# Attention's turns as pairs of 64 rows, the tail's second half an iteration later, ranks moved to other iterations

## The chip, the cores and the metric

The kernel runs on one core of a Trainium2 chip. The metric is the device time of one execution in microseconds (us). Five engines work side by side, each through its own queue in order: TensorE (PE, with its weight loads shown as PEld), VectorE (DVE), ScalarE (ACT), GpSimd (POOL) and SyncE (SP), which issues most DMAs. Matmuls write PSUM, and VectorE and ScalarE read it.

## The reference

Attention with a threshold under the row's maximum, then a gated mixture of experts (two of eight), then a dense layer of 2048 hidden units.

```python
scores = scale * np.matmul(q, k.transpose(0, 1, 3, 2))          # 4 batches, 8 heads, 576 x 576
thresh = np.max(scores, axis=-1, keepdims=True) - tau
scores = np.where(scores >= thresh, scores, -1000000000.0)
attn = np.exp(scores - np.max(scores, axis=-1, keepdims=True))
attn = attn / (np.sum(attn, axis=-1, keepdims=True) + 1e-09)
x = np.matmul(attn, v)                                          # 2304 tokens x 512
...
noisy_logits = x @ w_gate + np.log1p(np.exp(x @ w_noise)) * noise
out[mask] += top2_w * (np.maximum(x[mask] @ w1[e], 0.0) @ w2[e])  # both chosen experts e
...
g = np.maximum(h, 0.0) + alpha * np.minimum(h, 0.0)             # h = x @ w_in
return g @ w_out
```

## The kernel before, in words

The order of all instructions is written by hand: Python loops emit them, and each engine works through its own in that order.

Attention goes through 80 units (`units`). A unit is one pair of heads (`hp`) and one chunk of 128 queries of one batch, both heads of it, or a "t" unit: the 64 queries that are left over, with the two heads stacked on the 128 partitions (`nh(i)` is 2 or 1). The first 16 units are batch 0's chunks with the pair of heads as the outer loop (`SOLO`); from there on four units in a row, one for each pair, make up one tile of 128 tokens.

The main loop runs over iterations `i` and overlaps units: in iteration `i` the scores of unit `i+1` are multiplied (`s_mm`, two heads side by side in two halves of 64 rows of the array), the minimum of the negated scores of unit `i` is taken on VectorE (`d1`, `L358`), ScalarE takes the exponential (`a1`, `L369`) and the threshold (`thresh`), VectorE masks unit `i-1` (`d2`, `L382`), the masked exponentials of unit `i-2` (`it`) are turned on TensorE (`t_mm`: nine 128x128 transposes in a full unit, five in a "t" unit) and copied from PSUM by ScalarE (`a2`), and the outputs of unit `i-3` (`iv`) are multiplied (`pv`). The ninth turn is the "tail": the last 64 keys of both heads.

PSUM tiles of the tag "t" (`psum_t`) come from three buffers, which the turns, the turned rows of a finished token tile, its logits, their flip and the ranks share. A buffer is taken when its last reader is done.

Around a finished token tile the list `x_stages` places four steps in later iterations: `rows` (four turns, multiplied by 1/sum on VectorE, `L477`, and stored), `logits` (four small matmuls), `flip` (one turn) and `sum_`. The list `gating` does the same for groups of two or three tiles: noise, top two, `rank` (five matmuls of ones and a triangle), `place`, and the sends (`send`, indirect DMAs). An entry `(d, p, f)` means: `d` iterations later, at place `p`, where 0 is ahead of the outputs and 1 behind them.

ScalarE also rounds the next q and k (`split_hi`, `L289` and `L291`) and, from iteration 66 on, expert weights (`w_hi`, `L170`). Behind attention the experts and the dense layer follow, with TensorE working without pause.

Of the kernel before, what the change touches and what calls it, by code (L numbers as in the profile page):

```python
# [10 lines left out]
OP = mybir.AluOpType  # L11
# [22 lines left out]
def emit(tc, qt, kt, v, tau, wg, wn, noise, w1, w2, w_in, w_out, alpha, out):  # L34
# [8 lines left out]
    with (  # L43
# [192 lines left out]
        wcat, noise_t = cr([HP, 32]), cr([NT, E])  # L236
        lt_ring = Ring([cr([128]) for _ in range(3)])
# [10 lines left out]
        def load_consts():  # L248
            for h in range(2):
                for k, w in enumerate((wg, wn)):  # L250
                    sp.dma_start(wcat[h * 64:h * 64 + 64, :, h * 16 + k * 8:h * 16 + k * 8 + 8],
                                 w.rearrange("(c h p) e -> h p c e", h=2, p=64)[h])
            sp.dma_start(noise_t, noise)
            sp.dma_start(alpha_t, alpha)
# [134 lines left out]

        def t_mm(i, part):  # L390
            u = st[i]
            em = u["em"]
            emf = em.rearrange("p h s -> p (h s)")
            ps = psum_t()
            u["pt", part] = ps
            if part < 2:
                o = part * 640
                for j in range(4):
                    pe.transpose(ps[:, j * 128:j * 128 + 128], emf[:, o + j * 128:o + j * 128 + 128], ident)
            elif nh(i) == 2:  # L400
                pe.transpose(ps[:, :128], emf[:, 512:640], ident)
            else:
                pe.transpose(ps[:64, :128], emf[:, 512:576], ident)

        def a2(i, part):
            u = st[i]
            if part == 0:
                u["P"] = pt_ring()
            ps = u.pop(("pt", part))
            if part < 2:  # L410
                act.copy(u["P"][:, 4 * part:4 * part + 4].rearrange("p a b -> p (a b)"), ps)
            elif nh(i) == 2:
                act.copy(u["P"][:, 8], ps[:, :128])
            else:
                act.copy(u["P"][:64, 8], ps[:64, :128])
# [49 lines left out]
        def x_stages(T):  # L465
            g = {}

            def rows():
                x = xts[T]
                e = esum[T]  # L470
                dve.tensor_scalar(e, e, 1e-9, None, op0=OP.add)
                dve.reciprocal(e, e)
                ps = psum_t()
                for c in range(HP):
                    pe.transpose(ps[:, c * 128:c * 128 + 128], x[:, c], ident)
                xtok[T] = xtok_ring()
                dve.tensor_tensor(xtok[T].rearrange("p (h d) -> p h d", h=H), ps.rearrange("p (h d) -> p h d", h=H),  # L477
                                  e[:, :, None].to_broadcast([128, H, D]), op=OP.mult)
                sp.dma_start(xd[T * 128:T * 128 + 128], xtok[T])

            def logits():
                x = xts[T]
                ps = psum_t()
                for c in range(HP):
                    pe.matmul(ps[c * 32:c * 32 + 32, :128], wcat[:, c], x[:, c], start=True, stop=True,
                              skip_group_check=True)
                g["lt"] = lt_ring()
                act.copy(g["lt"], ps[:, :128])

            def flip():  # L490
                g["ps"] = psum_t()
                pe.transpose(g["ps"][:, :128], g["lt"], ident)

            def sum_():
                t = lt_ring()
                dve.tensor_tensor(t.rearrange("p (h j) -> p h j", h=H),
                                  g["ps"][:, :128].rearrange("p (h j) -> p h j", h=H),
                                  esum[T][:, :, None].to_broadcast([128, H, 16]), op=OP.mult)
# [10 lines left out]
        def gating(t0, t1):  # L509
# [90 lines left out]
            if 3 < t1 <= 12:  # L600
                plan = [(d, 1, f) for d, f in enumerate(first)] + [(5, 1, rank), (6, 0, place)]
                if t1 == FIRST:
                    plan.append((9, 0, close))
                return plan + [(6 + q, 1, lambda a=a: send(*a)) for q, a in enumerate(sends)]
            if t1 <= 15:
                plan = [(d // 2, 1, f) for d, f in enumerate(first)] + [(4, 1, rank), (5, 0, place)]
                return plan + [(5 + q // 2, 1, lambda a=a: send(*a)) for q, a in enumerate(sends)]
# [103 lines left out]
        for i in range(END):  # L711
            it, iv = i - DT, i - DT - 1
            tiles, outs = 0 <= it < NU, 0 <= iv < NU
            if tiles:
                t_mm(it, 0)
                a2(it, 0)
            if i < NU:
# [17 lines left out]
            if i + 1 < NU:  # L735
                s_mm(i + 1)
# [392 lines left out]
```

## Time and profile before

| | |
|---|---|
| timed runs | 1195.02, 1197.77 and 1198.08 us, median 1197.77 |
| the profiled execution's own time | 1204.04 us, of which its span (first to last instruction) is 1202.3 us |
| TensorE, matmuls | 1163.5 us busy, 97% of the span |
| VectorE, ScalarE, GpSimd | 588.4, 528.8 and 509.8 us busy |
| mean granted TensorE clock | 0.995 |

A busy time counts each moment in which at least one instruction of the engine ran. Matmuls overlap, and their ends are modelled, so a busy TensorE is not one at its peak. Line numbers such as L399 are those of the kernel before.

### The profile page before, as it was taken

Reading aid. Unit: us, or ns where it says so; the run is one execution under the profiler, and the core shown is the slowest. Engines: PE = TensorE matmul, PEld = TensorE weight load, DVE = VectorE, ACT = ScalarE, POOL = GpSimd, SP = SyncE. Lnnn points to the kernel's source line nnn. Section 1 sums busy time; section 2 is a strip of 40 time slices with the busy share of each in tenths; the row PEclk is TensorE's granted clock in tenths of the full one; section 3 lists DMA queues with packets and bytes.
Section 4 is the critical chain, followed back from the end, with each engine's and each line's share of the span. In section 5 each row is a group of like instructions: output and inputs, shape, how many; then the busy total and the mean of one; then the engine's idle time right before and its main releaser. Section 6 shows DMA issues by size and latency. Waiting matters only on the chain. (4 is left out here: it accounts for less than half of the span.)

```text
span 1202.3 us, 20313 instructions
## 1 busy us (share of the span) xinstructions
PE 1163.5 (97%) x7942; PEld 999.8 (83%) x7942; DVE 588.4 (49%) x1287; ACT 528.8 (44%) x1039; POOL 509.8 (42%) x553
## 2 busy tenths in 40 slices
PE   7998989999889999999999999999999999999997
PEld 6887777877778989888989898989888888888886
DVE  7978878799533433432534342345333333333222
ACT  7977868787524444444444354433111211211111
POOL 6736435643224544444444445546323332332221
PEclk9999999999999999999999999999999999999999
DMA  7323222142235555455555545542110100200001
GB/s 216 130 84 130 78 92 62 72 148 80 108 131 185 184 190 196 166 166 176 201 189 188 187 164 180 192 153 72 37 34 18 62 26 18 71 19 18 35 1 37
DMA packets 60597, 135.19 MB, mean 112 GB/s; under 512 B 9680, under 2 KB 10320, under 8 KB 60496
## 3 DMA queue, kind: packets, MB, share of 16 engines
q1 hardware_dynamic: 54448, 114.61, 28.1%
q0 software_dynamic: 5760, 18.88, 4.6%
q8 instruction: 64, 1.05, 0.3%
q14 instruction: 37, 0.30, 0.1%
q10 hardware_dynamic: 288, 0.34, 0.1%
HBM read 93.96 MB, written 39.85 MB: 111 GB/s over the span
## 5 line engine op out<-in xcount | busy, mean ns | idle before, releaser
L197 PE MATMUL ps_t<-m_v,m_pair 128*128 128x384 f32 (+2 forms) x1216 | 220.8, 318 | 1.2 <-DVE m_gate L208 1.2
L197 PEld LDWEIGHTS ps_t<-m_v,m_pair 128*128 128x128 f32 x1216 | 187.0, 190 | 9.8 <-DVE m_gate L208 1.8
L173 POOL TENSOR_TENSOR m_pair<-m_v,m_pair 128x1024 fp32r<-128x1024 f32 x55 | 134.8, 2452 | 137.8 <-ACT m_pair L170 137.5
L215 PE MATMUL ps_s<-m_pair,m_hh 128*128 128x512 f32 x528 | 175.6, 396 | 0.0
L954 DVE TENSOR_SCALAR m_tmp<-ps_t,alpha_t 128x512 f32<-128x512 f32 (+1 forms) x80 | 55.7, 696 | 216.9 <-PE ps_t L197 216.9
L208 DVE SCALAR_TENSOR_TENSOR m_gate<-ps_t,m_hh 128x384 fp32r<-128x384 f32 (+1 forms) x120 | 58.3, 493 | 153.8 <-ACT m_hh L207 153.7
L197 PE MATMUL ps_t<-m_v,m_early 128*128 128x256 f32 (+2 forms) x672 | 127.5, 321 | 1.3 <-ACT m_v L189 0.8
L382 DVE SCALAR_TENSOR_TENSOR m_hh<-m_tmp,sm,m_hh 128x576 f32<-128x576 f32 x144 | 127.2, 915 | 2.4 <-ACT sm L363 2.0
L215 PEld LDWEIGHTS ps_s<-m_pair,m_hh 128*128 128x128 f32 x528 | 99.2, 188 | 20.3
L959 POOL TENSOR_TENSOR m_v<-m_tmp,m_v 128x512 fp32r<-128x512 f32 x39 | 50.3, 1290 | 149.1 <-ACT m_v L958 149.1
L358 DVE TENSOR_SCALAR_CACHE_REDUCE m_tmp<-ps_s 128x576 f32<-128x576 f32 x144 | 103.6, 752 | 18.5 <-PE ps_s L347 15.8
L197 PEld LDWEIGHTS ps_t<-m_v,m_early 128*128 128x128 f32 x672 | 105.8, 189 | 6.6 <-ACT m_v L189 1.1
L369 ACT ACTIVATE m_hh<-m_tmp,sm 128x576 f32<-128x576 f32 x144 | 105.7, 783 | 10.9 <-DVE m_tmp L358 10.8
L347 PE MATMUL ps_s<-m_pair 64*128 64x288 f32 (+1 forms) x864 | 96.1, 321 | 12.9 <-DVE m_tmp L358 8.2
L215 PE MATMUL ps_s<-m_pair,m_gate 128*128 128x512 f32 x264 | 103.2, 391 | 0.0
L958 ACT CAST m_v<-m_tmp 128x512 fp32r<-128x512 f32 x39 | 24.2, 621 | 177.1 <-DVE m_tmp L955 177.1
L347 PEld LDWEIGHTS ps_s<-m_pair 64*128 64x128 f32 (+1 forms) x864 | 73.2, 194 | 27.9 <-DVE m_tmp L358 13.7
L978 PE MATMUL ps_s<-m_pair,m_v 128*128 128x512 f32 x396 | 95.9, 391 | 0.0
L207 ACT ACTIVATE m_hh<-ps_t 128x384 fp32r<-128x384 f32 (+1 forms) x120 | 51.9, 439 | 93.5 <-PE ps_t L197 92.2
L959 POOL TENSOR_TENSOR m_gate<-m_tmp,m_gate 128x512 fp32r<-128x512 f32 (+1 forms) x41 | 44.1, 1077 | 114.5 <-ACT m_gate L958 110.3
L978 PE MATMUL ps_s<-m_pair,m_gate 128*128 128x512 f32 x360 | 89.2, 393 | 0.0
L978 PEld LDWEIGHTS ps_s<-m_pair,m_v 128*128 128x128 f32 x396 | 73.9, 188 | 15.3
(226 smaller groups left out, 1994.2 us busy)
## 6 DMA issues: line engine op xcount, KB each, us to landing
m_v<-in_w_dram SPq DMA_DIRECT2D x64, 512.0 KB, 4.0
yg<-m_tmp SPq DMA_DIRECT2D x40, 256.0 KB, 3.6
m_tmp<-in_w_in_dram SPq DMA_DIRECT2D x16, 512.0 KB, 5.2
m_tmp<-in_w_out_dram SPq DMA_DIRECT2D x16, 512.0 KB, 5.7
m_v<-xg SPq DMA_DIRECT2D x20, 256.0 KB, 6.2
m_rows<-xg SPq DMA_DIRECT2D x20, 256.0 KB, 4.1
m_early<-in_kt_dram SPq DMA_DIRECT2D x15, 320.0 KB, 3.1
yg<-m_gate SPq DMA_DIRECT2D x18, 256.0 KB, 2.0
```

Of the source, the lines that this page charges most:

```text
L173: eng.tensor_tensor(WL[n], wraw.pop(n), f32(WH[n]), op=OP.subtract)
L197: pe.matmul(ps[:, :n], w[wc[d]][:, col:col + 128], x[xx][:, d, :n], start=(k == 0), stop=(k == 11))
L207: act.activation(h, ps, AF.Relu)
L208: dve.scalar_tensor_tensor(hs[1][:, f * n:f * n + n], ps, 0.0, f32(h), op0=OP.max, op1=OP.subtract)
L215: pe.matmul(ps, a[:, o:o + 128], ww[w][:, c:c + 512], start=(f == 0 and k == 0), stop=(f == nf - 1 and k == 2))
L347: pe.matmul(u["ps", h][:, x, :288], lhs, kk[r, o:o + 288], start=(k == 0), stop=(k == 2))
L358: dve.tensor_scalar(u["sp"][:, h].rearrange("p (a b) -> p a b", a=2), ps[:, :, :288], -0.125, None, op0=OP.mult, op1=OP.min, accum_out=u[" ...
L369: act.activation(u["em"][:, h], u["sp"][:, h], AF.Exp, bias=u["sm"][:, h:h + 1], scale=-1.0)
L382: dve.scalar_tensor_tensor(u["em"][:, h], u["sp"][:, h], sm[:, 2 + h:3 + h], u["em"][:, h], op0=OP.is_le, op1=OP.mult, accum_out=acc)
L954: dve.tensor_scalar(g, ps, 0.0, alpha_t[:, f:f + 1], op0=OP.min, op1=OP.mult)
L959: pool.tensor_tensor(h[:, n:2 * n], g, f32(h[:, :n]), op=OP.subtract)
L978: pe.matmul(ps, h[x][:, t * 128:t * 128 + 128], ww[w][:, c:c + 512], start=(f == 0 and k == 0), stop=(f == 15 and k == 2))
```

## The change

Every turn in attention is done as two turns of 64 rows each, side by side in the two row halves of the array, the way the scores are: `lo` gets queries 0 to 63, `hi` queries 64 to 127, in two PSUM tiles. All of a unit's turns are emitted at the start of the iteration and the scores right behind them. The tail's first half (`tail`) is turned there too, the second half, in the same PSUM tile, one iteration later (`t_mm(iv, 1)`), and copied then (`a2(iv, 2)`). The token tile's rows and the flip are turned in the same way and move ahead of the outputs. The logits take two steps of 64 columns in place of four of 32. Ranks come four iterations after their gating starts, with `place`.

```diff
+        def turn2(lo, hi, src):
+            r0, r1 = slice(0, 64), slice(64, 128)
+            pe.transpose(lo, src[r0], ident[r0, r0])
+            pe.transpose(hi, src[r1], ident[r1, r1])
...
         def t_mm(i, part):
...
-                for j in range(4):
-                    pe.transpose(ps[:, j * 128:j * 128 + 128], emf[:, o + j * 128:o + j * 128 + 128], ident)
...
+            if part == 0:
+                lo, hi, tail = [psum_t() for _ in range(3)]
+                u["pt"] = [lo, hi, tail]
+                for j in range(4 * nh(i)):
+                    if j == 4 * nh(i) - 1:
+                        pe.transpose(tail[:k, r0], emf[r0, 512:512 + k], ident[r0, r0])
+                    o = j * 128 + (128 if j > 3 else 0)
+                    c = slice(j * 64, j * 64 + 64)
+                    turn2(lo[:, c], hi[:, c], emf[:, o:o + 128])
             else:
+                two = pe.transpose(u["pt"][2][:k, r1], emf[r1, 512:512 + k], ident[r1, r1])
+                tc.add_manual_dep(two.ins, u["copied"].ins.name, ...)
...
         def a2(i, part):
...
             if part < 2:
-                act.copy(u["P"][:, 4 * part:4 * part + 4].rearrange("p a b -> p (a b)"), ps)
+                done = act.copy(P[:, :n, part * 64:part * 64 + 64],
+                                       ps[:, :n * 64].rearrange("p (a b) -> p a b", b=64))
+                u.setdefault("copied", done)
...
-            return [(0, 1, rows), (1, 1, logits), (2, 1, flip), (3, 0, sum_)]
+            return [(0, 0, rows), (1, 1, logits), (2, 0, flip), (2, 0, sum_)]
...
-                plan = [(d, 1, f) for d, f in enumerate(first)] + [(5, 1, rank), (6, 0, place)]
+                plan = [(d // 2, 1, f) for d, f in enumerate(first)] + [(4, 0, rank), (4, 0, place)]
...
+            if outs:
+                t_mm(iv, 1)
+                a2(iv, 2)
             if tiles:
                 t_mm(it, 0)
                 a2(it, 0)
+                a2(it, 1)
...
-            if tiles and nh(it) == 2:
-                t_mm(it, 1)
-                a2(it, 1)
-            if tiles:
-                t_mm(it, 2)
-                a2(it, 2)
+            if i + 1 < NU:
+                s_mm(i + 1)
```

The first place is TensorE's queue in an iteration of the first 16 units. Before, the turns (`L399`, the tail `L401`) stand ahead of the scores (`L347`) and the outputs (`L435`):

```order
L399 MATMUL ps_t<-ident,m_hh 128x128 [waits DVE_49,Activation_49]
L399 MATMUL ps_t<-ident,m_hh 128x128 x3
L401 MATMUL ps_t<-ident,m_hh 128x128 [waits Activation_49]
L347 MATMUL ps_s<-m_pair 128x288 [waits DVE_49] x2
L347 MATMUL ps_s<-m_pair 128x288 x10
```

And with the change, from the tail's first half (`L409`) on, with the last pair of turns (`L395`, `L396`), the scores (`L349`), the outputs (`L448`, `L450`) and the next iteration's first instruction, the tail's second half (`L414`):

```order
L409 MATMUL ps_t<-ident,m_hh 128x64 [waits Activation_49]
L395 MATMUL ps_t<-ident,m_hh 128x64
L396 MATMUL ps_t<-ident,m_hh 128x64
L349 MATMUL ps_s<-m_pair 128x288 [waits DVE_49] x2
L349 MATMUL ps_s<-m_pair 128x288 x10
L448 MATMUL ps_v<-m_last,m_v_72 64x128 x8
L450 MATMUL ps_v<-m_last,m_v_72 64x128 x2
L414 MATMUL ps_t<-ident,m_hh 128x64 [waits Activation_49]
```

The last pair of turns now stands behind an instruction that waits for ScalarE: the wait of `L409` is for the copy of the tail before it (`L428` below), since the two have one PSUM buffer.

The second place is ScalarE's queue in the same iterations. Before, a half's copy (`L411`), the two exponentials (`L369`), the other copies (`L411`, `L413`), the threshold (`L363`), the outputs' copy (`L453`):

```order
L411 COPY m_last<-ps_t 128x512 [waits PE_49,Activation_49]
L369 ACTIVATE m_hh<-m_tmp,sm_154 128x576 [waits DVE_49] x2
L411 COPY m_last<-ps_t 128x512 [waits PE_49,Activation_49]
L413 COPY m_last<-ps_t 128x128 [waits PE_49]
L363 ACTIVATE sm_154<-sm_154,taut 128x2
L453 COPY m_last<-ps_v 128x128 [waits PE_49]
```

And with the change, a rounding of k (`L293`) ahead of it:

```order
L293 CAST m_pair<-m_early 128x640 [waits DMAHW6_49]
L428 COPY m_last<-ps_t 128x128 [waits PE_49]
L424 COPY m_tmp<-ps_t 128x8x64 [waits PE_49,Activation_49] x2
L371 ACTIVATE m_hh<-m_tmp,sm_147 128x576 [waits DVE_49] x2
L365 ACTIVATE sm_147<-sm_147,taut 128x2
L466 COPY m_hh<-ps_v 128x128 [waits PE_49]
```

The tail's copy (`L428`, of the unit before) now comes first, and both halves' copies (`L424`) stand between it and the exponentials.

The third place is TensorE's queue in an iteration with a token tile's turned rows. Before, the rows (`L475`) come behind the outputs:

```order
L347 MATMUL ps_s<-m_pair 128x288 x10
L435 MATMUL ps_v<-m_last,m_v_73 64x128 x8
L437 MATMUL ps_v<-m_last,m_v_73 64x128 x2
L475 MATMUL ps_t<-ident,m_last 128x128 [waits DVE_49]
L475 MATMUL ps_t<-ident,m_last 128x128 x3
```

And with the change (the rows are turned by `L395` and `L396` too, from `m_last` here; three more pairs follow, then the outputs):

```order
L349 MATMUL ps_s<-m_pair 128x288 [waits DVE_49] x2
L349 MATMUL ps_s<-m_pair 128x288 x10
L395 MATMUL ps_t<-ident,m_last 128x64 [waits Activation_49]
L396 MATMUL ps_t<-ident,m_last 128x64 [waits Activation_49]
```

The rows now stand between the scores and the outputs, and wait for ScalarE's copies of the low and the high half, whose PSUM buffers they take.

## Rows read from the trace of the kernel before

**Rows 1.** The page's first part: busy us, share of the span, instructions.
```profile
PE 1163.5 (97%) x7942; PEld 999.8 (83%) x7942; DVE 588.4 (49%) x1287; ACT 528.8 (44%) x1039; POOL 509.8 (42%) x553
```

**Rows 2.** Windows, five stretches: busy PE, PEld, DVE, ACT, POOL (instructions), clock, DMA.
```profile
17.91:58.53 40.62, 40.55 (x494) 34.48 (x493) 37.75 (x99) 39.62 (x94) 25.55 (x39) 1.00 0.48 156
58.53:93.11 34.58, 33.53 (x417) 28.13 (x416) 26.92 (x73) 26.50 (x66) 14.72 (x36) 1.00 0.22 73
93.11:217.26 124.15, 114.09 (x1305) 92.22 (x1305) 103.81 (x311) 94.36 (x209) 63.47 (x110) 0.99 0.27 92
217.26:240.84 23.58, 23.47 (x285) 20.11 (x284) 17.79 (x58) 18.24 (x46) 14.21 (x32) 1.00 0.18 68
240.84:301.54 60.70, 56.38 (x654) 45.45 (x653) 56.37 (x146) 48.51 (x103) 24.24 (x32) 0.97 0.33 118
```

**Rows 3.** Timeline of PE, one iteration: start, length, instruction, count [idle before].
```profile
38.54 1.05 PE L347 MATMUL ps_s<-m_pair 64*128 64x288 f32 x12
39.52 1.09 PE L435 MATMUL ps_v<-m_tmp,m_v 128*64 128x128 f32 x16
...
40.77 1.09 PE L399 MATMUL ps_t<-ident,m_hh 128*128 128x128 f32 x8
...
41.90 0.40 PE L347 MATMUL ps_s<-m_pair 64*128 64x288 f32 x2
```

**Rows 4.** Timeline of ACT, parts of two iterations of that stretch.
```profile
35.43 1.48 ACT L369 ACTIVATE m_hh<-m_tmp,sm 128x576 f32<-128x576 f32 x2
36.78 0.61 ACT L411 COPY m_tmp<-ps_t 128x512 f32<-128x512 f32 x1
37.24 0.31 ACT L413 COPY m_tmp<-ps_t 128x128 f32<-128x128 f32 x1
37.40 0.35 ACT L363 ACTIVATE sm<-sm,taut 128x2 f32<-128x2 f32 x1
37.60 0.30 ACT L453 COPY m_hh<-ps_v 128x128 f32<-128x128 f32 x1
...
41.05 0.68 ACT L289 CAST m_pair<-m_early 128x576 fp32r<-128x576 f32 x1
41.62 0.59 ACT L411 COPY m_tmp<-ps_t 128x512 f32<-128x512 f32 x1
```

**Rows 5.** Windows, a group of four units with one token tile (units 36 to 39).
```profile
131.86:147.88 16.02, 15.15 (x179) 12.37 (x178) 13.77 (x47) 13.51 (x31) 8.16 (x15) 1.00 0.17 57
```

**Rows 6.** Groups by line, 0 to 420 us: count, busy, mean ns, idle before, releasers.
```profile
L170 ACT CAST m_pair<-m_v 128x1024 fp32r<-128x1024 f32 x12 | 12.5, 1045 | 0.0
L477 DVE TENSOR_TENSOR m_gate<-ps_t,es 128x512 f32<-128x512 f32 x18 | 12.4, 691 | 22.5 <-PE ps_t L475 19.3 <-PE ps_t L399 2.7
L413 ACT COPY m_last<-ps_t 128x128 f32<-128x128 f32 x32 | 9.1, 286 | 0.0
```

**Rows 7.** Timeline of PEld: the first two weight loads of a score batch.
```profile
41.90 0.19 PEld L347 LDWEIGHTS ps_s<-m_pair 64*128 64x128 f32 x2 [0.17 <-DVE m_hh L382]
```

**Rows 8.** Timeline of ACT and PE: a tail's turn that waits for a copy.
```profile
127.59 0.60 ACT L411 COPY m_tmp<-ps_t 128x512 f32<-128x512 f32 x1
...
128.24 0.33 PE L401 MATMUL ps_t<-ident,m_hh 128*128 128x128 f32 x1 [0.32 <-ACT m_tmp L411]
```

**Rows 9.** Timeline of PE and ACT: a copy that waits for matmuls.
```profile
123.00 0.42 PE L485 MATMUL ps_t<-m_hh,m_rows 128*32 128x128 f32 x8
...
123.51 0.27 ACT L488 COPY m_rows<-ps_t 128x128 f32<-128x128 f32 x1 [1.15 <-PE ps_t L485]
```

**Rows 10.** Timeline of PE: score batches of two "t" units.
```profile
77.04 1.04 PE L347 MATMUL ps_s<-m_pair 128*128 128x288 f32 x6
...
79.53 0.38 PE L347 MATMUL ps_s<-m_pair 128*128 128x288 f32 x1
```

**Rows 11.** Windows: a long iteration, and what follows; second figure PE, last but two clock.
```profile
160.00:163.40 3.40, 1.69 (x19) 1.30 (x17) 3.37 (x10) 1.75 (x3) 0.66 (x1) 1.00 0.37 148
163.50:166.90 3.40, 3.40 (x27) 3.04 (x26) 3.21 (x10) 1.50 (x5) 0.00 (x0) 0.50 0.02 5
```

More of the change, by code (lines that the diff above doesn't have):

```diff
@@ L235, in emit @@
         lg = cr([NT, 16])
-        wcat, noise_t = cr([HP, 32]), cr([NT, E])
-        lt_ring = Ring([cr([128]) for _ in range(3)])
+        wcat, noise_t = cr([HP, 64]), cr([NT, E])
+        lt_ring = Ring([cr([128]) for _ in range(2)])
         pool.iota(iota8, pattern=[[1, E]], base=0, channel_multiplier=0, allow_small_or_imprecise_dtypes=True)
@@ L250, in load_consts @@
                 for k, w in enumerate((wg, wn)):
-                    sp.dma_start(wcat[h * 64:h * 64 + 64, :, h * 16 + k * 8:h * 16 + k * 8 + 8],
-                                 w.rearrange("(c h p) e -> h p c e", h=2, p=64)[h])
+                    for c in range(HP):
+                        o = c % 2 * 32 + h * 16 + k * 8
+                        sp.dma_start(wcat[h * 64:h * 64 + 64, c, o:o + 8],
+                                     w[(2 * c + h) * 64:(2 * c + h) * 64 + 64])
             sp.dma_start(noise_t, noise)
@@ L408, in a2 @@
                 u["P"] = pt_ring()
[L409 removed]
+            P, n, ps = u["P"], 4 * nh(i), u["pt"][part]
             if part < 2:
[L411 to L413 removed]
+                done = act.copy(P[:, :n, part * 64:part * 64 + 64],
+                                       ps[:, :n * 64].rearrange("p (a b) -> p a b", b=64))
+                u.setdefault("copied", done)
             else:
[L415 removed]
+                act.copy(P[:64 * nh(i), 8], ps[:64 * nh(i), :128])
         vps, xts, esum = {}, {}, {}
@@ L483, in logits @@
                 ps = psum_t()
-                for c in range(HP):
-                    pe.matmul(ps[c * 32:c * 32 + 32, :128], wcat[:, c], x[:, c], start=True, stop=True,
-                              skip_group_check=True)
+                for k in range(2):
+                    for h in range(2):
+                        pe.matmul(ps[h * 64:h * 64 + 64, :128], wcat[:, 2 * h + k], x[:, 2 * h + k],
+                                  start=(k == 0), stop=(k == 1), skip_group_check=True)
                 g["lt"] = lt_ring()
@@ L599, in gating @@
             first = [exp_, one_plus, log_, noisy, top2]
-            if 3 < t1 <= 12:
-                plan = [(d, 1, f) for d, f in enumerate(first)] + [(5, 1, rank), (6, 0, place)]
+            if t1 <= 15:
+                plan = [(d // 2, 1, f) for d, f in enumerate(first)] + [(4, 0, rank), (4, 0, place)]
                 if t1 == FIRST:
[L603 to L607, printed above, removed]
+                    plan.append((8, 0, close))
+                return plan + [(5 + (q if 3 < t1 <= 12 else q // 2), 1, lambda a=a: send(*a)) for q, a in enumerate(sends)]
             plan = [(0, 1, f) for f in first] + [(1, 2, rank), (1, 2, place)]
```

38 lines of the change are left out of this document (18 added, 20 removed).

## The prediction

> **What bounds the kernel now.** I read the page first: TensorE is busy 97% of the span [rows 1], so a microsecond is won only where TensorE waits or does less, and the change touches attention alone. Then I cut attention, by the starts of score batches, into five stretches [rows 2]: iterations 4 to 15 (batch 0's full query chunks), the tail units ("t") with their neighbours, the 29 iterations 27 to 55, the second tail units, the last 15. Behind them TensorE is full, so a shift of attention's end goes through to the end. What I looked for in each stretch is which engine ends an iteration.
>
> In iterations 4 to 15 it is TensorE: score batches start 3.36 us apart and TensorE has no pause but its tiling switches [rows 3]: turns to scores 1.13, scores to outputs 0.98, outputs to the next turns 1.25. ScalarE is close behind. From row to row [rows 4] it needs 1.35 us for two exponentials, 0.46 for a 512-column copy (two of them), 0.16 for the 128-column tail copy, 0.20 for the threshold: 2.63 us; with the copy of the outputs (128 columns too, 0.16) and a rounding of q or k (0.57 for q, by its columns 0.63 for k), 3.36 to 3.42. Both engines are full there.
>
> In iterations 27 to 55 a group of four units with one turned tile takes 16.02 us when nothing else comes in between; TensorE is busy 15.15 of them, VectorE 13.77, ScalarE 13.51 [rows 5]. The loss is a chain: VectorE waits for the turned rows (`L477`), because they are queued behind the outputs; over attention this wait is 22.5 us for 18 tiles, 1.25 each [rows 6].
>
> **The change, part by part.**
>
> *Turns.* Nine turns of 128 columns become nine slots of 64 columns, two row halves side by side. No row shows such a pair. Bounds: half of 0.11 us (1.13 less the switch of 0.20, over nine, is 0.10 to 0.11), if the halves run side by side as the scores' halves do; or 0.11 again. The rows are nearer to the first: two 64-row loads of the scores end within 0.19 us together [rows 7]. With 0.055, and with turns and scores in one tiling (a switch of about 0.2 less), TensorE needs 0.50 + 0.98 + 1.25 = 2.73 us for what took 3.36. If that were all, 64 full iterations would give 40 us where TensorE binds.
>
> The Trainium skill, "TensorE: Matmul & The Clock Gate", section "LDWEIGHTS (loading the stationary operand)", says that a load costs by its columns, not its rows, so a 64-row load is as long as a 128-row one; by that, and without overlap, 18 loads would take twice what 9 took. Two loads of 64 rows end in 0.19 us here [rows 7], so the trace does not have them one after the other; I keep a small chance for the rule as a rival.
>
> *A new wait.* The order shows what the change adds: the tail's tile stays in PSUM from one iteration to the next, so the first half of the tail's turn (`L409`) waits for ScalarE's copy of the tail before, and behind `L409` in TensorE's queue stands the last pair of turns, for which ScalarE's next instruction, the copy of the low half, waits. ScalarE therefore stands still inside every iteration, by: tail copy 0.29 long (`L413`, mean [rows 6]), 0.05 to TensorE's start (copy ends 128.19, TensorE starts 128.24 [rows 8]), 0.27 for a 64-column turn (0.33 for 128 columns after such a wait [rows 8], less 0.055), 0.055 for the last pair, 0.09 from TensorE's end to ScalarE's start (123.42 to 123.51 [rows 9]). That is 0.76 from start to start where 0.16 was needed: 0.60 us of ScalarE idle per iteration, whatever the speed of the turns. ScalarE's plain iteration becomes 2.63 + 0.60 = 3.23; TensorE's own circle (0.50 + 0.98 + 1.25, and 0.36 until the next tail can be copied) is 3.09, VectorE's at most 3.12 (37.75 us busy in 12.1 periods of 3.36 [rows 2]), so ScalarE is now the bound.
>
> *Iterations 4 to 15.* 3.23 + 0.16 = 3.39, plus a rounding of 0.6 in ten of the twelve: 46.7 us where the row [rows 2] has 40.62: **+6.1**.
>
> *Tail units, 16 of them.* TensorE binds (score batches 2.49 apart with one flip in it [rows 10]). Five turns of 0.11 go; in their place stand the result of the second half (0.36), its copy 0.29, 0.05, three slots 0.16, and a switch to the scores' 128-row tiling that was not there (0.15), less the switch 0.1 saved behind the outputs: 0.9 for 0.55, so 0.3 to 0.35 more each, 5 us; turned rows, logits and flips of six tiles cost some 0.2 less each: **+3.6**.
>
> *Iterations 27 to 55.* Rows are turned ahead of the outputs now. They need the low and the high half's PSUM tiles back, the latter 1.86 us after the tail copy (0.76, then 0.46 to the second copy, which lasts about 0.6 like the 0.60 in [rows 8], then 0.05), so VectorE's stall shrinks to about 0.9 and lies where ScalarE binds anyway. Per group: 3.23 + 0.46 (copy of a tile); 3.23 + 0.6 (rounding), which covers the turned rows; logits, TensorE's circle with 0.44 for two accumulated steps, 3.53, and 0.25 since VectorE is late after the rows; 3.23 + 0.6. Sum 15.1 against 16.02: 0.9 for 7.25 groups, 6.5 us. The remaining 8.0 us of the stretch (124.15 less 7.25 times 16.02) are three gatings and a spell of low clock; ranks in their own iterations cost a switch or two each, and I take 5 for 8. Together **-9.5**.
>
> *Last 15.* ScalarE also rounds seven weight tiles of 1.05 us (`L170` [rows 6]), which its slack hid and which now add. 15 times 3.23, 1.4 and 0.5 for three tiles' copies, 7.3 of weights, 0.6 of gating, 1.2 less for three short iterations: 57.1, with 4 to 6 for iterations in which TensorE or VectorE is late: 61 to 63 against 60.70: **+1**.
>
> *The rest.* VectorE's multiplication of a tile in two halves costs 0.1 to 0.3 more (0.69 whole [rows 6]; a half takes no less than 0.35 and I take no more than 0.5): up to 5 us over 18 tiles, hidden where VectorE is busy 3.58 us of each of the 29 iterations (103.81 [rows 2]) and ScalarE needs 3.78; if that slack is gone it costs all 5. Sixteen small weight loads for four on SyncE's queue stand behind the inputs of the first iterations; the next ones are needed in iteration 9, 36 us on.
>
> Sum: 6.1 + 3.6 - 9.5 + 1 = +1.2 us on the profiled execution's 1204.04. The median of the three timed runs is 1197.77, 6 us lower, and the difference is carried over: 1199.
>
> **Rivals.**
> *No measurable change (forecast).* What TensorE gives up, ScalarE's wait takes back. Own range 1195 to 1203. Chance 0.40.
> *Faster.* The wait for the tail does not bind from iteration 27 on, because ScalarE would wait there for VectorE's minima anyway (if these come later than 1.7 us after the tail copy). Then VectorE is the bound: 103.81 us busy in the stretch, 2 for the split multiplications, 3 of stalls, 109 for 124.15; the last 15 give 2. With +9.7 from the first two: -7, 1191. For it: VectorE is the busiest engine but TensorE there [rows 2]; against it: its 3.58 us per iteration hold gating and rows already and lie under ScalarE's 3.78. Chance 0.25.
> *Slower.* ScalarE as the bound takes everything in full: gating's exponentials, weight roundings, and VectorE's bursts of gating that now hold up the scores and through them the next tail. If the iterations with roundings and logits come to over 4.0 us instead of 3.8, the middle gives 4 instead of 9.5 and the last 15 cost 5: +10, 1208. Chance 0.28.
> *The clock.* Where an iteration left TensorE busy only 1.69 of 3.40 us, the granted clock was 0.50, its level of 1.2 GHz, in the stretch behind it [rows 11]; such a spell of 3.4 us costs about 1.7. TensorE will be busy 2.7 of each 3.4 to 4 us, more than in that row; if spells come anyway, four to six cost 7 to 10: 1208. Chance 0.05. The Trainium skill, same page, "Part 4: PE-mode transpose", says that turns do not count as work for the clock in the same way; by that this change, which lengthens the iterations around the other matmuls, would bring such spells. Iterations 4 to 15, with nine turns in each, have a clock of 1.00 [rows 2], which neither proves nor breaks it.
> *Loads one after the other.* 18 slots of 0.11 give 2.0 us of turns; TensorE's circle is then 4.2 to 4.6 in 64 iterations, 40 us more: 1240. Chance 0.02.
>
> **Numbers.** This kernel's runs lie 3 us apart, so 0.3% (3.6 us, 1194.2 to 1201.4) is what can be told from none. Of the forecast's 0.40, 0.06 lies above and 0.01 below; of the faster rival 0.03 stays inside, of the slower ones 0.01. Faster 0.23, same 0.37, slower 0.40. The range 1190 to 1210 takes in both main rivals and leaves the loads and the ends.
>
> **What would show it.** ScalarE's copy of the low half should start about 0.76 us after the tail copy, released by TensorE, in nearly every iteration, with TensorE's last pairs released by ScalarE's tail copy. Score batches should lie 3.4 (no rounding) and 4.0 us (rounding) apart in iterations 4 to 15; turns in pairs 0.055 apart; `L477`'s successor should wait under 1 us per tile. It is wrong if the low half's copy is not held, if pairs lie 0.11 apart, or if the middle stretch falls under 110 us or stays above 120.

## The result, and the profile after

The changed kernel took 1208.24 us (median of six runs, 1206.70 to 1209.72) where the kernel before took 1196.37 (six runs, 1194.17 to 1198.08): a ratio of 1.0097, 95% interval 1.0083 to 1.0111, about 12 us slower. The number lies inside the predicted range (1190 to 1210), 9 us above the predicted time. But the forecast was no measurable change, and by the prediction's own measure (0.3% can be told from none) this kernel is slower. The profiled execution took 1206.98 us, as the timed runs do.

The page's first part of the changed kernel, to be read beside [rows 1]; columns are busy us, share of the span, instructions:

```profile
PE 1147.5 (95%) x8688; PEld 987.2 (82%) x8688; DVE 598.6 (50%) x1323; ACT 532.8 (44%) x1055; POOL 504.5 (42%) x553
```

TensorE does 16 us less work and the kernel takes longer: the time lies in waits. The same five stretches as in [rows 2], in the changed kernel; after the window come span, busy PE, PEld, DVE, ACT, POOL with their instructions, granted clock, DMA share, GB/s:

```profile
16.76:64.31 47.55, 37.45 (x604) 31.31 (x602) 40.81 (x101) 41.11 (x94) 25.58 (x41) 1.00 0.43 132
64.31:101.97 37.66, 34.53 (x503) 27.95 (x500) 26.15 (x78) 26.65 (x71) 12.39 (x34) 1.00 0.22 75
101.97:217.25 115.28, 104.18 (x1604) 86.05 (x1602) 110.19 (x326) 95.49 (x210) 62.04 (x113) 1.00 0.30 102
217.25:244.41 27.16, 25.05 (x349) 20.32 (x347) 19.39 (x66) 18.81 (x50) 12.46 (x33) 1.00 0.14 52
244.41:305.06 60.65, 51.01 (x794) 42.56 (x794) 55.38 (x150) 48.31 (x105) 25.67 (x29) 0.97 0.34 116
```

In iterations 4 to 15 TensorE was busy 40.55 of 40.62 us before; now it is busy 37.45 of 47.55, and ScalarE (41.11) stands still for 6.4. Where it stands still is in its timeline (start, length, instruction, count, [idle before, releaser]):

```profile
44.46 1.07 ACT L424 COPY m_tmp<-ps_t 128x512 f32<-128x512 f32 x2 [0.48 <-PE ps_t L395]
45.42 1.46 ACT L371 ACTIVATE m_hh<-m_tmp,sm 128x576 f32<-128x576 f32 x2
...
47.73 0.28 ACT L428 COPY m_tmp<-ps_t 128x128 f32<-128x128 f32 x1
48.49 0.59 ACT L424 COPY m_last<-ps_t 128x512 f32<-128x512 f32 x1 [0.48 <-PE ps_t L395]
```

and in TensorE's, at the same moment:

```profile
46.50 0.22 PE L396 MATMUL ps_t<-ident,m_hh 64*128 64x64 f32 x1
46.51 0.22 PE L395 MATMUL ps_t<-ident,m_hh 64*128 64x64 f32 x1
46.56 0.22 PE L396 MATMUL ps_t<-ident,m_hh 64*128 64x64 f32 x1
...
48.06 0.27 PE L409 MATMUL ps_t<-ident,m_hh 64*128 64x64 f32 x1 [0.96 <-ACT m_tmp L428]
48.07 0.27 PE L396 MATMUL ps_t<-ident,m_hh 64*128 64x64 f32 x1
```

ScalarE copies the tail at 47.73; its next copy, the low half, starts at 48.49, 0.76 later, because TensorE's last pair stands behind the tail's turn (`L409`), which starts when that tail copy ends. In 79 of the 80 units the low half's copy follows the tail's in this way, released by TensorE, 0.65 to 1.03 us from start to start in all but two. The pairs themselves lie 0.06 us apart. Over attention these groups sum it up (count, busy us, mean ns, idle before and its releasers):

```profile
L424 ACT COPY m_tmp<-ps_t 128x512 f32<-128x512 f32 (+1 forms) x80 | 39.6, 547 | 20.2 <-PE ps_t L395 20.2
L424 ACT COPY m_last<-ps_t 128x512 f32<-128x512 f32 (+1 forms) x80 | 39.6, 547 | 21.4 <-PE ps_t L395 21.0 <-PE ps_t L396 0.4
L409 PE MATMUL ps_t<-ident,m_hh 64*128 64x64 f32 (+1 forms) x80 | 20.5, 256 | 23.7 <-ACT m_tmp L428 15.5 <-ACT m_last L428 7.7
L491 DVE TENSOR_TENSOR m_gate<-ps_t,es 128x256 f32<-128x256 f32 x36 | 13.6, 419 | 7.5 <-PE ps_t L396 4.2 <-PE ps_t L395 1.6 <-DMA xg<-m_gate,posi 0.4
```

ScalarE waits 41.6 us for TensorE in 80 units, TensorE 23.2 for ScalarE. In return VectorE's wait for turned rows is 7.5 us where it was 22.5 [rows 6].

### The profile page after: what moved, and what is told of

Read it like the earlier page. It is cut to its first block, busy times and chain, and to the rows that moved or that the text cites. A ratio compares the mean times of both kernels' runs of the same rounds, so it can differ in the third digit from the quotient of the medians.

```text
span 1205.3 us, 21846 instructions
## 1 busy us (share of the span) xinstructions
PE 1147.5 (95%) x8688; PEld 987.2 (82%) x8688; DVE 598.6 (50%) x1323; ACT 532.8 (44%) x1055; POOL 504.5 (42%) x553
## 5 line engine op out<-in xcount | busy, mean ns | idle before, releaser
L384 DVE SCALAR_TENSOR_TENSOR m_hh<-m_tmp,sm,m_hh 128x576 f32<-128x576 f32 x144 | 130.3, 937 | 5.8 <-ACT sm L365 5.7
L349 PE MATMUL ps_s<-m_pair 64*128 64x288 f32 (+1 forms) x864 | 97.3, 319 | 11.0 <-DVE m_tmp L360 5.7
L349 PEld LDWEIGHTS ps_s<-m_pair 64*128 64x128 f32 (+1 forms) x864 | 76.0, 194 | 18.5 <-DVE m_tmp L360 10.8
```

The source lines that it names most:

```text
L349: pe.matmul(u["ps", h][:, x, :288], lhs, kk[r, o:o + 288], start=(k == 0), stop=(k == 2))
L384: dve.scalar_tensor_tensor(u["em"][:, h], u["sp"][:, h], sm[:, 2 + h:3 + h], u["em"][:, h], op0=OP.is_le, op1=OP.mult, accum_out=acc)
```

## The experiments

The theory: each iteration's hand-over of the tail's PSUM tile (ScalarE copies, TensorE turns, ScalarE copies) is what the change pays, some 0.6 us of ScalarE per iteration; turned rows ahead of the outputs are what it gains, in the middle. Rivals: the wait is covered by VectorE or by TensorE's own circle; the profile of before was no fair base; the low clock.

Medians and ratios to the kernel before, from rounds on one chip each (the first four rows on one, the next four on a second, the last four on a third):

| run | us | before | ratio (95%) |
|---|---|---|---|
| e1 before, again | 1195.16 (one run) | 1195.23 | |
| e2 tail whole, behind the scores | 1192.29 | 1195.23 | 0.9974 (0.9960 to 0.9987) |
| e3 old turns, new places | 1190.43 | 1195.23 | 0.9957 (0.9941 to 0.9972) |
| e4 new turns, rows behind | 1227.81 | 1195.23 | 1.0280 (1.0260 to 1.0299) |
| e5 tail between halves | 1208.93 | 1202.50 | 1.0051 (1.0036 to 1.0066) |
| e6 changed, GpSimd behind d2 | 1227.00 | 1202.50 | 1.0202 (1.0184 to 1.0219) |
| e7 tail whole, GpSimd behind d2 | 1199.80 | 1202.50 | 0.9977 (0.9966 to 0.9989) |
| e8 old turns, GpSimd behind d2 | 1192.00 | 1202.50 | 0.9918 (0.9904 to 0.9932) |
| e9 rows ahead alone | 1194.27 | 1195.54 | 0.9989 (0.9976 to 1.0001) |
| e10 flips and ranks alone | 1193.51 | 1195.54 | 0.9984 (0.9973 to 0.9995) |
| e11 = e3 again | 1190.02 | 1195.54 | 0.9956 (0.9944 to 0.9968) |
| e12 = e8 again | 1190.22 | 1195.54 | 0.9961 (0.9948 to 0.9974) |

**e1, the kernel before once more.** No edit. Expected:

> The kernel before, unchanged, for a second profile: the prediction's sum stood on a profiled execution of 1204.04 us, 6 to 8 us above the timed runs. If that execution was an odd one, this one takes 1194 to 1199, and the stretch where the old one lost 6 us can be named: its three spells at half clock (3.4 us long, about 1.7 us each) would then be fewer, or the 29 iterations 27 to 55 shorter than 124.15. Rival: a profile always costs this kernel the 6 us (about 1204 again), and then the two profiles compare as they stand (+3.0) and the timed runs' +11.9 has another source.

It took 1195.16. The five stretches:

```profile
17.95:58.55 40.60, 40.55 (x493) 34.47 (x493) 37.71 (x99) 39.64 (x94) 25.49 (x38) 1.00 0.50 156
58.55:93.16 34.61, 33.55 (x417) 28.13 (x416) 26.96 (x73) 26.55 (x66) 14.75 (x36) 1.00 0.22 73
93.16:212.78 119.62, 112.04 (x1305) 90.68 (x1305) 103.70 (x311) 95.28 (x210) 62.95 (x110) 1.00 0.28 96
212.78:236.15 23.37, 23.37 (x285) 20.10 (x283) 17.29 (x58) 17.90 (x45) 12.76 (x32) 1.00 0.18 69
236.15:295.05 58.90, 54.87 (x654) 44.10 (x653) 56.26 (x147) 48.55 (x103) 26.03 (x32) 1.00 0.34 121
```

Beside [rows 2], the first, second and fourth stretches agree to about 0.2 us; the middle is 4.53 shorter and the last 1.80. Score batch by score batch the two executions agree to some 0.05 us but for a few iterations: 31 lost 0.45 in the first profile, 42 and 43 lost 1.42 and 1.57, 45 and 46 together 1.2, 73 lost 1.57. So the first profile was no fair base: it had lost 4.5 us in the middle, where the prediction booked its gain, and 1.8 in the last 15. Whether it was an odd execution or an ordinary one of another chip stays open: the record does not name its chip, and on one of the three chips of the experiments (e5 to e8) every run of the kernel before took 1200 to 1205 us. The granted clock shows a part of the loss (43 and 73); what lengthened 42, 45 and 46 is not shown. The same times as [rows 11], now in the undisturbed execution:

```profile
160.00:163.40 3.40, 3.11 (x39) 2.42 (x38) 2.93 (x11) 2.90 (x7) 0.99 (x1) 1.00 0.32 123
163.50:166.90 3.40, 3.40 (x44) 2.89 (x43) 1.68 (x6) 3.38 (x8) 0.00 (x0) 1.00 0.00 0
```

TensorE busy 3.11 of 3.40 us, and the clock stays at 1.00 (2.4 GHz); in the first profile it was busy 1.69 and the clock fell to 0.50 (1.2 GHz) behind that. Against this base the change costs, stretch by stretch, +6.95, +3.05, -4.34, +3.79, +1.75; iteration 4 starts 1.2 earlier. The last score batch of attention starts 10.0 us later (305.06 for 295.05), the kernel ends 11.8 later.

**e2, the wait taken away.** The tail is turned in one piece of 128 rows behind the scores, ahead of the outputs; no tile stays over.

```
     if part == 0:
-        lo, hi, tail = [psum_t() for _ in range(3)]
-        u["pt"] = [lo, hi, tail]
+        lo, hi = [psum_t() for _ in range(2)]
+        u["pt"] = [lo, hi]
         for j in range(4 * nh(i)):
-            if j == 4 * nh(i) - 1:
-                pe.transpose(tail[:k, r0], emf[r0, 512:512 + k], ident[r0, r0])
...
     else:
-        two = pe.transpose(u["pt"][2][:k, r1], emf[r1, 512:512 + k], ident[r1, r1])
-        tc.add_manual_dep(two.ins, u["copied"].ins.name, ...)
+        u["pt"].append(psum_t())
+        pe.transpose(u["pt"][2][:k, :128], emf[:, 512:512 + k], ident)
...
-    if outs:
-        t_mm(iv, 1)
-        a2(iv, 2)
...
         s_mm(i + 1)
+    if tiles:
+        t_mm(it, 1)
     if i < NU:
         thresh(i)
+    if tiles:
+        a2(it, 2)
```

> The changed kernel with the tail's turn in one piece of 128 rows, behind the scores and ahead of the outputs of the same iteration, so that neither TensorE's last pair nor ScalarE's copy of the low half stands behind ScalarE's copy of the tail before; everything else as changed. Theory (ScalarE's 0.60 us per iteration behind the tail's PSUM tile is what the change pays): the low half's copy follows without the 0.76 from start to start, iterations 4 to 15 take 3.39 with a rounding and 3.12 without (VectorE), 40 to 41 us in all for 47.55; the two tail stretches 2 to 6 less; the middle, where VectorE is busy 110.19 of 115.28 us, only 1 to 3 less; the last 15 by 2 to 4. Sum 12 to 17 less: 1191 to 1196. Rival (the wait is covered anyway, VectorE or the pairs themselves set the time): 1203 to 1209.

It took 1192.29, 16 less than the changed kernel and 0.26% less than before. Its stretches:

```profile
16.50:56.13 39.63, 38.72 (x590) 31.82 (x588) 35.78 (x97) 38.56 (x91) 25.59 (x36) 1.00 0.51 159
56.13:93.41 37.28, 35.59 (x493) 28.72 (x490) 26.90 (x82) 27.71 (x77) 14.35 (x40) 0.95 0.22 76
93.41:208.47 115.06, 107.49 (x1573) 87.18 (x1573) 108.31 (x324) 94.64 (x210) 62.12 (x110) 0.99 0.30 102
208.47:231.97 23.50, 23.50 (x341) 19.77 (x338) 19.83 (x66) 18.03 (x51) 14.39 (x35) 1.00 0.15 58
231.97:289.78 57.81, 53.07 (x782) 43.20 (x777) 53.57 (x152) 47.62 (x106) 25.75 (x29) 0.97 0.35 123
```

The first stretch gives 7.92 back and is bounded by ScalarE (38.56 of 39.63), which now waits for nothing ahead of the two halves' copies, as the groups of this stretch say:

```profile
L421 ACT COPY m_tmp<-ps_t 128x512 f32<-128x512 f32 x12 | 7.3, 740 | 0.0
L421 ACT COPY m_last<-ps_t 128x512 f32<-128x512 f32 x12 | 7.2, 714 | 0.0
```

The second tail stretch gives back 3.66 of the 3.79 that the change had cost. So the stay-over of the tail is the cost, in these two stretches in full and at the expected size. The last 15 give back 2.84. The middle hardly moves (1 to 3 less was expected), and the 0.95 in the second row is new: one iteration there took 6.42 us where e3's takes 3.86. What stands ahead of it and in it:

```profile
59.40:62.70 3.30, 2.18 (x20) 1.53 (x19) 2.36 (x6) 3.30 (x11) 2.37 (x4) 1.00 0.00 0
...
62.70:66.10 3.40, 3.40 (x37) 2.95 (x38) 2.25 (x7) 1.43 (x6) 2.00 (x8) 0.51 0.38 105
```

TensorE busy 2.18 of 3.30 us, then half clock: the picture of [rows 11].

**e3, the places alone.** The kernel before, its turns of 128 columns and its tail untouched, with rows, flips and ranks where the change puts them.

```
-    return [(0, 1, rows), (1, 1, logits), (2, 1, flip), (3, 0, sum_)]
+    return [(0, 0, rows), (1, 1, logits), (2, 0, flip), (2, 0, sum_)]
...
-    if 3 < t1 <= 12:
-        plan = [(d, 1, f) for d, f in enumerate(first)] + [(5, 1, rank), (6, 0, place)]
...
+    if t1 <= 15:
+        plan = [(d // 2, 1, f) for d, f in enumerate(first)] + [(4, 0, rank), (4, 0, place)]
```

> The kernel before with one part of the change alone: turned rows ahead of the outputs, flip and sum one iteration after the logits, ranks one place earlier with place in the same iteration; turns of 128 columns, the tail and the logits' steps as before. Theory (the middle's 8.9 us came from taking VectorE's wait for the turned rows away, not from the shorter turns): iterations 27 to 55 fall from 124.15 to about 116 to 118, bounded by TensorE's idle time there of 10.06; 4 to 15 stay at 40.6; total 6 less than before, 1188 to 1192. Rival (TensorE full, so that rows ahead of the outputs only delay the outputs; the gain needs the shorter turns): 1195 to 1198.

It took 1190.43, and 1190.02 when run again (e11): faster than before by 0.4% both times. Two of its stretches:

```profile
58.22:92.22 34.00, 33.67 (x417) 28.05 (x416) 27.20 (x73) 26.20 (x65) 14.08 (x37) 1.00 0.25 86
...
92.22:208.83 116.61, 112.24 (x1306) 91.90 (x1305) 107.64 (x309) 94.78 (x211) 59.28 (x110) 0.99 0.29 100
```

The middle falls by 3.0 against e1, the first tail stretch by 0.6, and 4 to 15 stay at 40.63. Most of the middle's gain is here without the turns. How far one profile carries is seen in e11, the same kernel once more, whose middle took 114.82. Units 44 to 47, which half clock touches in none of these profiles, are a better measure: 16.08 us in e1, 15.38 in the changed kernel, 14.76 in e2, and 14.66 here (14.65 in e11). There the turns add nothing to the places.

**e4, rows and flips behind the outputs again,** in the changed kernel.

```
-    return [(0, 0, rows), (1, 1, logits), (2, 0, flip), (2, 0, sum_)]
+    return [(0, 1, rows), (1, 1, logits), (2, 1, flip), (2, 1, sum_)]
```

> The changed kernel with turned rows and flips behind the outputs again, as before the change; pairs, tail, ranks and everything else as changed. Theory (rows ahead of the outputs are what keeps VectorE going): its wait for the turned rows is back at about 1.2 us a tile, VectorE is full in the middle, so iterations 27 to 55 go from 115.28 to 122 to 125 and the kernel to 1214 to 1220. Rival (ScalarE, held by the tail, sets the iteration and covers the wait): 1206 to 1210.

1227.81, more than expected. VectorE's waits in the middle (total, times, longest), and that stretch:

```profile
DVE m_rows L514 <- PE ps_t L414: 14.8, 8, 3.3
DVE m_gate L491 <- PE ps_t L414: 5.8, 6, 1.4
DVE m_gate L491 <- PE ps_t L396: 2.4, 1, 2.4
```

```profile
105.27:235.45 130.18, 112.05 (x1606) 91.19 (x1602) 105.21 (x326) 95.75 (x210) 57.67 (x109) 0.94 0.27 92
```

Rows cost 8.2 us (the expected 1.2 a tile), but the sum, which has to follow its flip in the same iteration since the flip holds two of the three PSUM tiles, costs 14.8 more; the stretch grows by 14.9 in all, at a clock of 0.94, and how much of that is the clock was not separated. The expectation had priced the first wait only.

**e5, the wait moved off ScalarE.** In the changed kernel the tail's first half goes between the halves of the last pair.

```
-    if j == 4 * nh(i) - 1:
-        pe.transpose(tail[:k, r0], ...)
...
-    turn2(lo[:, c], hi[:, c], emf[:, o:o + 128])
+    pe.transpose(lo[:, c], emf[r0, o:o + 128], ident[r0, r0])
+    if j == 4 * nh(i) - 1:
+        pe.transpose(tail[:k, r0], ...)
+    pe.transpose(hi[:, c], emf[r1, o:o + 128], ident[r1, r1])
...
-    u.setdefault("copied", done)
+    u["copied"] = done
```

> The changed kernel with one instruction moved by one place: the first half of the tail's turn stands between the two halves of the last pair, not ahead of it, and the second half waits for the copy of the high half. TensorE still waits for ScalarE's copy of the tail before; but the copy of the low half no longer stands behind that, and ScalarE has 0.46 us of it to do while TensorE answers. Theory (it is ScalarE's standing still that costs, not TensorE's wait): ScalarE's idle falls from 0.60 to about 0.15 an iteration, iterations 4 to 15 from 47.55 to 41.5 to 43, the last 15 by 1 to 3; the middle, where VectorE is as full, by under 1; total 1195 to 1199. Rival (TensorE's wait for the tail is the bound): no change, 1205 to 1209.

Iterations 4 to 15, and the copies of both halves in it:

```profile
16.75:61.24 44.49, 38.70 (x606) 32.38 (x604) 38.65 (x101) 41.30 (x95) 26.14 (x40) 1.00 0.46 142
```

```profile
L425 ACT COPY m_last<-ps_t 128x512 f32<-128x512 f32 x13 | 7.3, 594 | 0.9 <-PE ps_t L410 0.7 <-ACT m_last L425 0.2
L425 ACT COPY m_tmp<-ps_t 128x512 f32<-128x512 f32 x12 | 6.7, 595 | 0.2 <-PE ps_t L410 0.2
```

ScalarE waits 1.1 us in this stretch where the changed kernel's waits 5.7 ahead of the same copies. Iterations without a rounding fall from 3.39 to 2.93, the 0.46 of the copy; those with one from 3.97 or 4.02 to between 3.47 and 3.79, by 0.2 to 0.5. So it is ScalarE's standing still that costs, and in this stretch the rival (TensorE's wait, which is still there) is out. The 44.49 misses the expected 41.5 to 43 by iteration 4 alone, which took 6.23 us where the changed kernel's took 4.59: TensorE worked at half pace there (16 matmuls of the outputs take 1.97 us, 1.09 in the changed kernel), though the record of the granted clock shows no drop. The total decides nothing, since 1208.93 lies in the rival's range: on this chip the kernel before took 1202.50, and the profiled execution ran 0.97 and 0.94 of full clock in the middle and the last 15:

```profile
97.81:217.65 119.84, 106.91 (x1604) 88.28 (x1602) 108.49 (x324) 95.27 (x210) 61.20 (x109) 0.97 0.29 98
...
244.39:306.42 62.03, 50.95 (x792) 42.83 (x792) 55.28 (x150) 48.62 (x105) 26.05 (x29) 0.94 0.33 114
```

**e6, e7, e8, GpSimd's subtraction behind VectorE's masking pass,** in the changed kernel, in e2 and in e3. The reason was this, in the changed kernel's middle (VectorE, then GpSimd):

```profile
133.84 0.76 DVE L360 TENSOR_SCALAR_CACHE_REDUCE m_tmp<-ps_s 128x576 f32<-128x576 f32 x1
...
134.51 1.44 DVE L384 SCALAR_TENSOR_TENSOR m_hh<-m_tmp,sm,m_hh 128x576 f32<-128x576 f32 x1
...
135.88 1.41 DVE L384 SCALAR_TENSOR_TENSOR m_hh<-m_tmp,sm,m_hh 128x576 f32<-128x576 f32 x1
```

```profile
134.47 2.21 POOL L301 TENSOR_TENSOR m_pair<-m_early,m_pair 128x320 fp32r<-128x320 f32 x2 [1.52 <-ACT m_pair L293]
```

The edit, the same in all three:

```
+    last[0] = dve.scalar_tensor_tensor(u["em"][:, h], ...)      (in d2)
...
-    pool.tensor_tensor(lo[:, c], raw[:, c], f32(hi[:, c]), op=OP.subtract)
+    sub = pool.tensor_tensor(lo[:, c], raw[:, c], f32(hi[:, c]), op=OP.subtract)
+    if o == 0 and last[0] is not None:
+        tc.add_manual_dep(sub.ins, last[0].ins.name, ...)
```

> The changed kernel, with one wait more: GpSimd's subtraction of the low part waits until VectorE's masking pass of the unit is done, so that it runs beside VectorE's minima and not beside the next masking pass. In the middle a masking pass takes 1.34 us in 16 of 59 cases, those beside a subtraction, and 0.82 else, 8 us in all. Theory (in the middle ScalarE with its 0.60 us of waiting, 95.49 busy and 17.4 waiting of 115.28, is as full as VectorE with 110.19): VectorE's busy time falls by 4 to 7, the middle by at most 3, iterations 4 to 15 not at all; 1204 to 1208. Rival (VectorE alone sets the middle): it falls to 108 to 110, and the kernel to 1200 to 1203.

> The kernel with the tail's turn in one piece (1192.29) and the same wait of GpSimd's subtraction for VectorE's masking pass. Theory (without ScalarE's wait, VectorE alone sets the middle, and the passes beside subtractions, 12 of 1.33 us there, are part of that): VectorE's busy time there falls from 108.31 to 102 to 104, the middle from 115.06 to 109 to 112; 1186 to 1189. Rival (ScalarE or TensorE, 107.49 busy, sets the middle): 1190 to 1193.

> The kernel before with the changed places of rows, flips and ranks (1190.43), turns of 128 columns, and the same wait of GpSimd's subtraction. TensorE is busy 112.24 of 116.61 us of the middle there, VectorE 107.64. Theory: VectorE's busy time falls by 5 to 7, but TensorE's 112.24 stands: the middle 113 to 115, the kernel 1187 to 1190, and the kernel with pairs and the same wait is faster than this one by 2 to 4, which is then what the pairs are worth. Rival (VectorE is not what ends iterations here): 1190 to 1192.

The middle of e6, of e7 and of e8:

```profile
104.72:229.63 124.91, 107.42 (x1604) 88.14 (x1602) 105.35 (x328) 95.46 (x210) 58.00 (x111) 0.97 0.27 94
```

```profile
94.22:212.29 118.07, 108.80 (x1572) 88.70 (x1572) 104.75 (x325) 92.81 (x207) 57.31 (x108) 0.97 0.29 99
```

```profile
92.32:208.73 116.41, 111.69 (x1305) 91.59 (x1305) 103.04 (x311) 94.25 (x210) 57.40 (x109) 0.99 0.30 100
```

VectorE was relieved as meant (110.19 to 105.35, 108.31 to 104.75, 107.64 to 103.04), and none of the three came out as its theory had it. e6 became slower than either theory had it. In iteration 4, which takes 7.19 us where it took 4.59, the low part is needed at once and ends 0.9 later (18.80 for 17.91), and the scores wait for it; the rest of the loss there is TensorE at half pace, as in e5, where GpSimd has no wait. Behind that, iterations 6 to 15 have the changed kernel's periods to 0.01 us, and units 44 to 47 take 15.30 for 15.38. That much fits the theory: VectorE is not what holds the changed kernel. The rest of e6's loss comes with a clock that was at 0.50 for 24 us of attention (3.4 in the changed kernel); why is not shown. In e7 units 44 to 47 take 14.21 us where e2's take 14.76; the total (1199.80, above both of its ranges, on the chip where the kernel before takes 1202.5) does not show that gain, with 14 us of attention at half clock. e8's middle is e3's, and so are its units 44 to 47 (14.65).

e8's ratio (0.9918) seemed to say otherwise. So e3 and e8 were run once more, side by side on a third chip.

**e9 to e12, the places taken apart, and the two best beside each other.** e9 is the kernel before with `(0, 0, rows)` and the rest as it was; e10 has the other new places and `(0, 1, rows)`; e11 is e3, e12 is e8.

> The kernel before with the turned rows ahead of the outputs and nothing else. Theory (the places' gain, ratio 0.9957 to before, is VectorE's wait for turned rows taken away): iterations 27 to 55 about 117 for the 119.62 of the undisturbed profile, the rest unchanged; ratio to before 0.996 to 0.998. Rival (the ranks and flips in their own iterations give it): 0.999 to 1.001.

> The kernel before with the flip, the sum and the ranks at their changed places and the turned rows behind the outputs as before. Theory (rows are what counts): 0.998 to 1.001 of before. Rival (ranks and flips give it): 0.995 to 0.997.

> The kernel before with the changed places of rows, flips and ranks, once more, now beside the next one on one chip, since its ratio (0.9957) and that of the kernel with GpSimd's wait (0.9918) come from chips on which the kernel before took 1195 and 1202. Here 0.995 to 0.997 if the ratio carries from chip to chip.

> The same with GpSimd's subtraction behind VectorE's masking pass. The two profiles have the same middle (116.61 and 116.41), so by the profiles the wait gains nothing: within 0.1% of the run beside it. Rival (the ratios are what counts, and the wait gains 0.4%): 0.4% below the run beside it.

e11 and e12 differ by 0.2 us: the wait gains nothing, and the ratios of the second chip (e5 to e8), where the kernel before took 7 us more and e8 less than 2 more, don't carry to the others. e9's middle, and the wait for turned rows over attention in e1 and in e9:

```profile
91.97:206.27 114.30, 109.83 (x1305) 89.32 (x1305) 106.22 (x311) 94.38 (x210) 63.96 (x110) 1.00 0.30 100
```

```profile
L477 DVE TENSOR_TENSOR m_gate<-ps_t,es 128x512 f32<-128x512 f32 x18 | 12.5, 692 | 20.3 <-PE ps_t L475 17.4 <-PE ps_t L399 2.4
```

```profile
L477 DVE TENSOR_TENSOR m_gate<-ps_t,es 128x512 f32<-128x512 f32 x18 | 12.5, 692 | 7.4 <-PE ps_t L475 4.7 <-DMA xg<-m_gate,posi 1.6 <-DVE es L472 0.3
```

Rows ahead of the outputs, and nothing else, take 5.3 us off the middle (more than expected) and 12.9 off VectorE's wait, as the theory says. But the timed gain is 0.11%, its interval just reaching 1: the runs of e9 lie between 1190.69 and 1197.11, and in the profiled one two of the last iterations take 6.45 and 6.17 us where e3's take 3.74 and 4.67. Flips and ranks alone give 0.16%. In units 44 to 47 the two parts add up: 15.00 us with the rows ahead (e9), 15.73 with flips and ranks moved (e10), 14.66 with both (e3), against e1's 16.08; so three quarters of that gain are the rows. In the timed runs only both together are steady, at 0.44%. Why e9 falls to half clock in the last iterations and e3 does not is left open.

## Why the prediction was right or wrong

Its range held, and that owes much to its width, which took in both main rivals. Its forecast, no measurable change at 1199, did not: the change costs 1%, clear of noise. The mechanism it named is there, to the digit; what failed is the base from which the middle's gain was taken, and the size of the tail units.

*Turns in pairs, 0.055 us each.* Right: 0.06. The rival of loads one after the other is out. The second half of one pair and the first half of the next start 0.00 to 0.01 us apart (`L396` at 46.50, `L395` at 46.51), so a pair takes one place, not two. The Trainium skill, "TensorE: Matmul & The Clock Gate", section "LDWEIGHTS (loading the stationary operand)", has a load cost by its columns, not its rows. The trace agrees: a half load of 64 rows and 128 columns takes 139 ns in the mean (596 loads of `L395`), a whole one of 128 rows took 142 (576 loads of `L399` in the kernel before). So the rule is not what was wrong with the rival; its other premise, loads one after the other, is.

*The new wait, 0.76 from start to start.* Right to the digit (47.73 to 48.49), and e2 and e5 show that it is the cost: without it iterations 4 to 15 fall to 39.63.

*Iterations 4 to 15, +6.1.* +6.95; the periods are 3.39 and 3.97 to 4.02, as worked out, but for iteration 4 (4.59) and 15 (4.20). The first four iterations gave 1.2, which the sum left out.

*Tail units, +3.6.* Mis-sized: +3.05 and +3.79, 6.8 together. The stay-over costs 3.66 in the second stretch (e2), 0.46 for each of eight tail units, where 0.30 to 0.35 for sixteen was taken. In the first stretch the same 3.66, less the 0.61 that the places save there (e3), is the 3.05 measured, though no run shows the two terms alone. VectorE's sums do wait for their flips there (5.1 us), but they wait as long in e2 (4.8), where the stretch, without the excess of the one iteration of 6.42, is about as long as before the change.

*The middle, -9.5.* The stretch came out at 115.28 where 114.65 was forecast, partly by luck: of the groups priced at 15.1, units 44 to 47 took 15.38, and units 36 to 39, those of [rows 5], 16.12, with VectorE busy 15.43 us in them where it was 13.77; so the rest of the stretch must have been cheaper than the 5 that were booked. The step that failed is the base: the 124.15 of [rows 2] held 4.5 us that e1 does not have. Against e1 the middle gained 4.34. The prediction booked 3 of a surplus of 8.0 us as gating and low clock that the change would save; in e1, where units 36 to 39 take 16.03, the same working leaves 3.4 in all, less than the 5 that it let stand.

*Last 15, +1.* 60.65 is just under the 61 to 63 forecast; but against e1's 58.90 it costs 1.75 where 1 was booked.

*The sum.* "The difference is carried over" is the sentence that was wrong. The 6 us between the profiled execution and the timed runs were not spread evenly over the kernel (4.5 and 1.8 of them lay in two stretches), and not common to both kernels: the changed kernel's profile is no slower than its timed runs. With the forecast lengths of the stretches against e1's, the same working gives 6.1 + 3.6 - 5.0 + 2.8 = +7.5, and 1203; what is left is mostly the tail units (3.2) and 1.8 behind attention.

*The rivals.* The slower one gave 1208, which is what was measured, but by luck: its gain of 4 in the middle stood against 124.15 and meant 120 us for the stretch, which took 115.28, and its 5 in the last 15 were 1.75. The dearer tail units, and the 6 us taken off for the first profile, made up for both. The faster one is out: its condition, that the wait does not bind from iteration 27 on, is refuted by units 44 to 47, which take 0.6 us less in e2 than in the changed kernel; its 109 us for the middle were 115.28. The clock: in attention the changed kernel has one spell of 3.4 us at half clock (at 257.5), where the first profile of the kernel before has two and e1 none; four to six were the rival's condition, so it is out for this kernel; but it came in e2 and e4 to e7. The Trainium skill's rule that turns do not count as work for the clock in the same way (same page, "Part 4: PE-mode transpose") is neither shown nor refuted by this: those kernels have shorter turns and other waits at once.

## What to carry to other kernels

A profile's own time far above the timed runs is a warning about that profile: find in which stretch the surplus lies, best with a second profile of the same kernel on the same chip, before a gain is booked there. A PSUM tile that lives across iterations tied two engines' queues together here; place the instruction that waits for its release behind everything that the other engine needs next, or better, let the tile live and die within one iteration (e2). And try the parts of a change apart: here the moved rows and ranks alone (e3) beat the kernel before by 0.4% and the changed one by some 1.4% (by their ratios, from two sets of runs), and the new turns, even without the stay-over (e2), added nothing to the total: they save 1.0 us in iterations 4 to 15 and 1.1 in the last 15, and the profile of e2 has 10 us of attention at half clock where e3's has 3.4.

## What the runs showed of the hardware

- VectorE's masking pass takes 0.82 us, and 1.41 to 1.44 beside GpSimd's subtraction in the lines above (2.92 once, beside the larger subtraction of expert weights), while its pass over PSUM takes 0.75 either way. The Trainium skill, "SBUF — State Buffer", section "SBUF: two separate sides", says that a VectorE operation with two SBUF inputs and a GpSimd operation share one port pair, which one of them holds while the other is blocked; the trace agrees. In the totals it cost nothing that could be seen: e12, which takes it away, is within 0.2 us of e11.
- Some of the kernels with pairs were at half clock for longer. In the profiled executions, between 20 and 420 us of the span, the granted clock was 0.50 for 0 to 10 us in the kernels with whole turns (e1, e3, e8 to e12, before), for 7 in the changed kernel, and for 17 to 34 in e2 and e4 to e7. With one profile of each this is no rule, and why the changed kernel has so little of it is not shown; e2's runs spread over 7.4 us, e3's over 2.8.
- In e5 and e6 TensorE worked at half pace in iteration 4 (16 matmuls of the outputs in 1.97 us for 1.09), with a recorded granted clock of 1.00: there the record alone does not show the pace.
- The kernel before takes 1195 to 1196 us on two chips of the experiments and 1202.5 on the third, while e3 with GpSimd's wait takes 1190 and 1192: a ratio measured on one chip can be 0.4% off on another.
